# Another order of six units, and projections and weight-gradient pieces paced by a running sum

## The chip, the cores and the metric

One core of one Trainium2 chip runs the kernel as one program. The time is device microseconds. Before the change it is 910.07 us, the median of two runs (909.61 and 910.52). The engines are named as the profile names them: PE (TensorE, matmuls and transposes), ACT (ScalarE), DVE (VectorE), POOL (GpSimd) and SP, which issues DMAs.

## The reference

Forward and backward of a gated mix of two branches over 2048 tokens of width 512, all in bf16: `g = sigmoid(sum(x * gate_w))`, out = `g * A(x) + (1 - g) * B(x)`. A is sliding-window attention with 32 heads of width 16 and a window of 256 keys:

```
scores = einsum("bhqd,bhkd->bhqk", q, k) * Dh**-0.5
mask   = (i - j >= 0) & (i - j < 256)
p      = softmax(where(mask, scores, -1e9));  o = p @ v;  a = o @ wo
```

B is a gated feed-forward layer of width 1376 (`h = relu(x W_gate) * (x W_up)`, `b = h W_down`). The outputs are the mix and the gradients of x and of the six weights, for a given `grad_out`.

## The kernel before

The kernel has three stages. The feed-forward stage comes first, the attention stage (forward and backward in one sweep, from about 250 to 710 us) second, and a last stage makes the output and the gradient of x. The change touches the attention stage alone.

**Passes, blocks, units, turns.** The attention stage makes four passes c = 0 to 3, the four "head groups", of eight heads each. A pass goes over 16 blocks j of 128 queries. A block meets three key blocks: its own (role d, the diagonal), the one before (role m, the middle, wholly inside the window) and the one before that (role f, the far one). Each is handled in two halves of four heads, so a block is six units (two for j = 0, four for j = 1), and a pass is 90 units. One loop iteration n, a turn, starts unit n and carries older units on:

- `front`, turn n: PE makes the scores ST (128x512), ACT takes their exponential, POOL masks it for roles d and f (L695, L698);
- `front_dp`, turn n+1: PE makes dPT, the gradient of the probabilities;
- `gradp`, turn n+2: DVE multiplies the two (L712);
- `rowsum`, turn n+4: PE sums over keys into BA, eight small matmuls (L721, L723), and after a block's last unit ACT copies BA out (L727) and POOL makes the block's small tiles in four later turns;
- `flip`: the unit's two tiles are transposed for the key-side gradients. Roles d and m go through one DMA transpose per pair of halves, issued by SP. Role f goes through PE in turn n+4: eight transposes into a tile pt, 0.44 us of PE, copied out by ACT and DVE in turn (L72, L74). In pass 3 part of role m goes through PE too;
- `cd_piece`: PE adds finished blocks into CD, the gradients of k and v (L541, L544).

**Fill-in work.** While a group of four blocks runs, the next group's projections are made in six parts (`project_parts`): Q and dO (four matmuls of 512 columns each into a tile pp, evicted by DVE, L147 and L74, then spread by four DVE copies, L120), a DMA transpose, K and V (pp evicted by ACT, L72, then two masked copies on DVE, L169), and the transposes of K and V (ptp, evicted by DVE in two copies, L191 and L192). The gradient of wqkv of pass c-1 is made during pass c by `grad_parts`, 16 pieces of four matmuls each (wps, 0.65 us). Four pieces form one accumulation, so its tile is taken by the first piece and given back after the fourth. In passes 1 and 2 this tile comes from the ring TR, in pass 3 from the ring M.

**PSUM.** The eight banks are: M, four buffers (ST, dPT, and wps of pass 3); CD, one; BA, one; TR, two. TR serves pt, pp, ptp and, in passes 1 and 2, wps.

**What sets the order.** Instructions are written out by hand, turn by turn. A number `credit` rises by a fixed amount per turn and falls with each piece of fill-in work; a projection part or a gradient piece is written when credit allows. `held` is true while an accumulation has pieces left. While it is true, the next piece goes first, and the condition for a projection part asks for `not held`.

Of the kernel before, what the change touches and what calls it, by code (L numbers as in the profile page):

```python
# [22 lines left out]
def kernel(  # L23
# [32 lines left out]
    DC = D // P  # L56
# [3 lines left out]
    NTG = S // TGW  # L60
# [43 lines left out]
    NP = P // 32  # L104
# [7 lines left out]
    if True:  # L112
# [5 lines left out]
        def spread(gi, k):  # L118
            rows = slice(32 * k, 32 * k + 32)
            nc.vector.tensor_copy(zt[gi % ZB][rows, :, k, :, :].rearrange("p w t q -> p w (t q)"),  # L120
                                  proj[groups[gi]]["z"][rows, :, :])
# [76 lines left out]
    with ExitStack() as p1, tc.manual_schedule():  # L198
# [43 lines left out]
        half = TPG // 2  # L242
# [105 lines left out]
        for fc in range(FC):  # L348
            for tg in range(NTG):
                k = Step()  # L350
# [97 lines left out]
        for n in range(N1 + 8):  # L448
# [29 lines left out]
            if at(6):  # L478
                f = weights(at(6))
# [34 lines left out]
    if True:  # L514
# [68 lines left out]
        def clear(name):  # L583
            nc.gpsimd.memset(W6[(name, FC - 1)][0:FC * P - F, :], 0.0)
# [8 lines left out]
        def turns(name, src, k0, k1, tag):  # L593
            full, end = src.shape[1] // P, -(-src.shape[1] // P)
            ks = range(k0, min(k1, full))
            sets = [list(ks[i:i + 2]) for i in range(0, len(ks), 2)] + ([[full]] if k0 <= full < min(k1, end) else [])
            return [lambda s=s: turn_w(name, src, s, tag, s[0] - k0) for s in sets]

        def loads(name, src, k0, tag):
            def one(k):  # L600
                if (tag, "t") not in W6:
                    W6[(tag, "t")] = slot(tag)
                load_rows(name, src, k, W6[(tag, "t")][:, k - k0, :])
            return [lambda k=k: one(k) for k in range(k0, min(k0 + 4, FC))]
# [8 lines left out]
        def load_gw():  # L613
            nc.sync.dma_start(gw_b[:], gate_w.partition_broadcast(P))

        plan = {2: [load_gw], 5: turns("wqkv", A_wqkv, 0, 4, "p0"), 7: turns("wqkv", A_wqkv, 4, 8, "p1"),
                11: turns("wqkv", A_wqkv, 8, 12, "p2"),
                12: turns("Wg", B_W_gate, 0, 4, "x0") + turns("Wg", B_W_gate, 4, 8, "d0"),
                13: turns("Wg", B_W_gate, 8, 12, "x1") + turns("Wu", B_W_up, 0, 4, "d1") + [lambda: clear("Wg")],
                14: turns("Wu", B_W_up, 4, 8, "x2") + turns("Wu", B_W_up, 8, 12, "d2"),  # L620
                15: loads("Wd", B_W_down, 0, "x3") + [lambda: clear("Wu")] + loads("Wd", B_W_down, 4, "d3") + loads("Wd", B_W_down, 8, "p3") + [load_wo]}
# [35 lines left out]
        units = []  # L657
        for c in range(DC):
            for j in range(NT):
                kbs = [k for k in (j - 1, j, j - 2) if k >= 0]  # L660
                for half in range(2):
                    order = kbs if half or len(kbs) < 3 else [kbs[0], kbs[2], kbs[1]]
                    for ki, kb in enumerate(order):
                        u = Unit()
                        u.c, u.j, u.kb, u.half = c, j, kb, half
                        u.first = ki == 0 and half == 0
                        u.last = ki == len(kbs) - 1 and half == 1
                        u.role = ("d", "m", "f")[j - kb]
                        u.pair = u.role == "d" or (u.role == "m" and (c < DC - 1 or j in (3, 5, 7, 9)))
                        u.own = u.role == "f"  # L670
                        u.dma = u.pair or (u.role == "m" and half == 0 and (c < DC - 1 or j < 10))
                        units.append(u)
        NU = len(units)

        pairs = {}
# [172 lines left out]
        with tc.manual_schedule():  # L848
            ev = {}
            cdq = []  # L850
            bgq = []
            prq = []
# [3 lines left out]
            n = 0  # L856

            held = False
            fed = 1
            early = []  # L860
            late = []

            def background():
                f, more = bgq.pop(0)
                store = f()
                if store is not None:
                    copies.append(store)
                    if len(copies) > 2 or gi + 2 >= len(groups):
                        ev.setdefault(n + 2, []).append(("dma", flush))
                return more  # L870

            def flush():
                while copies:
                    copies.pop(0)()

            def pieces():
                nonlocal credit
                most = 2 if len(cdq) > 6 or (len(cdq) > 1 and cdq[1][5] and cdq[1][0] <= n and cdq[1][2] < NT - 1) else 1
                if u is not None and u.c == DC - 1 and u.j > 9 and w is not None:
                    most = 2 if w.dma else 1 if len(cdq) > 3 or cdq and cdq[0][5] else 0  # L880
                for _ in range(most):
                    if cdq and cdq[0][0] <= n:
                        cd_piece(*cdq.pop(0)[1:])
                        credit -= 0.2

            while n <= NU + LAG or ev or cdq or bgq:
                now = ev.pop(n, [])
                u = units[n] if n < NU else None
                if u is not None:
                    gi = u.c * NTG + u.j // TPG  # L890
                    if u.first and u.j == 0:
                        sts[u.c] = st.tile([P, NT, 4, P], BF, tag="rows_st", name="rows_st")
                    if u.first and u.j % TPG == 0:
                        if gi + 1 < len(groups):
                            prq = project_parts(*groups[gi + 1]) if gi else second
                            due = n + sum(2 * min(3, j + 1) for j in range(u.j, u.j + TPG)) - 3
# [24 lines left out]
                w = units[n - LAG] if LAG <= n < NU + LAG else None  # L921
# [28 lines left out]
                if n >= NU:  # L950
                    if bgq:
                        held = background()
                    elif n > NU + 1:
                        for _ in range(2):
                            if len(S2["grads"]) > DC:
                                S2["grads"].pop(0)()
                elif held and credit > 0.3:
                    held = background()
                    credit -= 0.65
                elif prq and not held and ((credit > 0.4 and n > fed + 1) or due - n <= len(prq)):  # L960
                    fed = n
                    credit -= (0.44, 0.86, 0.86, 0.1, 0.86, 0.86)[len(prq) - 1]
                    prq.pop(0)()
                    if len(prq) == 4:
                        for k in range(NP):
                            ev.setdefault(n + 1 + k, []).append(("dve", lambda gi=gi, k=k: spread(gi + 1, k)))
                        ev.setdefault(n + 1, []).append(("dma", flush))
                    if not prq:
                        late += plan.get(gi + 1, [])
                elif bgq and len(prq) <= 2 and credit > 0.3:  # L970
                    held = background()
                    credit -= 0.65
# [164 lines left out]
```

## Time and profile before

| quantity | us |
|---|---|
| median of the two runs | 910.07 |
| profiled execution, its own time | 911.05 |
| its span | 909.4 |
| PE busy | 895.0 (98%) |
| DVE / ACT / POOL busy | 511.8 / 441.3 / 491.7 |
| granted PE clock | 1.00 of full speed |

| pass | starts at us | lasts us |
|---|---|---|
| 0 | 251.7 | 101.9 |
| 1 | 353.6 | 115.5 |
| 2 | 469.1 | 115.9 |
| 3 | 585.0 | to about 703 |

The passes' starts are the starts of their first ST. The matmul rows are pipelined. A row of 128x512 reads 378 ns, while such matmuls that follow each other start 215 ns apart. So for PE this document reads the steps from start to start: 215 ns for 512 columns, 161 for 384 (wps), 55 for a transpose, 25 for the small ones of BA and CD. A step that is longer than its matmul's own is a wait of PE, and is called a stall below.

### The profile page before, as it was taken

What the parts mean: (1) busy time and instruction counts of PE and PEld (TensorE: products, weight loads), DVE (VectorE), ACT (ScalarE), POOL (GpSimd) and SP (SyncE); (2) the same over time, 40 slices, a digit from 0 to 9 for tenths busy, and PEclk for the clock granted to TensorE, in tenths of its full rate; (3) what the DMA queues carried; (4) which work ended last, traced back from release to release, by engine and by line L of the source; (5) the groups of instructions that cost most, each with busy time, mean ns of one, the idle gap of its engine ahead of it and who ended that gap; (6) DMA issues with size and microseconds to landing.
All of it is one profiled execution on the core that took longest, in us unless ns stands there. A gap on an engine that the chain in (4) does not pass through costs nothing.

```text
span 909.4 us, 26127 instructions
## 1 busy us (share of the span) xinstructions
PE 895.0 (98%) x10711; PEld 566.7 (62%) x10711; DVE 511.8 (56%) x952; ACT 441.3 (49%) x778; POOL 491.7 (54%) x937
## 2 busy tenths in 40 slices
PE   9999999999989999999999999999999999999998
PEld 5555656655657777667776677766777644444445
DVE  4433334324468887678886788876787222333223
ACT  6422232222278777667776677766788211100001
POOL 4644545545267778767777567875677312222221
PEclk9999999999999999999999999999999999999999
DMA  9998879999799999999999989999999998777731
GB/s 301 203 194 186 197 179 207 211 207 216 180 143 158 180 188 194 184 175 156 177 185 187 180 161 182 187 182 184 184 185 186 235 269 227 186 181 185 182 86 46
DMA packets 505575, 169.06 MB, mean 186 GB/s; under 512 B 433456, under 2 KB 504336, under 8 KB 505456
## 3 DMA queue, kind: packets, MB, share of 16 engines
q1 hardware_dynamic: 484816, 145.51, 86.8%
q10 hardware_dynamic: 19008, 17.31, 7.2%
q0 software_dynamic: 1632, 4.59, 1.4%
q8 instruction: 83, 1.36, 0.6%
q14 instruction: 36, 0.29, 0.1%
HBM read 32.28 MB, written 36.24 MB: 75 GB/s over the span
## 4 chain that ended last, share of the span: by engine, by line
PE 80%; DMA 5%; DVE 4%; POOL 3%; issue 3%; SPq 2%; ACT 2%; ACTq 0%; POOLq 0%; DVEq 0%
PE dxps L1062 8%; PE ST L683 8%; PE dPT L707 7%; PE pt L750 6%; PE wps L412 5%; PE wps L637 5%; PE dxps L1066 4%; PE CD L541 4%; PE bps L1035 4%; PE BA L721 4%; PE pp L133 4%; PE dps L414 3%; PE ups L363 3%; PE gps L363 2%; PE CD L544 2%
## 5 line engine op out<-in xcount | busy, mean ns | idle before, releaser
L683 PE MATMUL ST<-z,K 128*128 128x512 bf16 x360 | 135.8, 378 | 2.6 <-DVE PPm L712 1.2
L707 PE MATMUL dPT<-z,V 128*128 128x512 bf16 x360 | 136.0, 378 | 1.9 <-DVE Pd L712 0.5
L695 POOL TENSOR_SCALAR_AFFINE_SELECT PPd<-PPd 128x512 bf16<-128x512 bf16 x126 | 80.0, 635 | 86.7 <-ACT PPd L693 86.7
L377 POOL TENSOR_TENSOR hT<-rg,upm 128x512 bf16<-128x512 bf16 x44 | 51.8, 1176 | 116.0 <-DVE upm L375 104.3
L412 PE MATMUL wps<-dgu_r,x_r 128*128 128x256 bf16 (+1 forms) x704 | 103.9, 270 | 1.8 <-DVE wst L74 1.8
L712 DVE TENSOR_TENSOR PPd<-PPd,dPT 128x512 bf16<-128x512 bf16 x126 | 85.4, 678 | 18.3 <-PE dPT L707 9.1
L698 POOL TENSOR_SCALAR_AFFINE_SELECT Pu<-Pu 128x512 bf16<-128x512 bf16 x112 | 71.9, 642 | 31.8 <-ACT Pu L693 30.7
L412 PEld LDWEIGHTS <-x_r 128*128 128x128 bf16 x704 | 68.4, 98 | 33.1 <-issue 2.6
L712 DVE TENSOR_TENSOR Pd<-Pu,dPT 128x512 bf16<-128x512 bf16 x112 | 76.3, 681 | 21.5 <-POOL Pu L698 10.6
L693 ACT ACTIVATE PPd<-ST 128x512 bf16<-128x512 f32 x126 | 76.1, 605 | 22.0 <-PE ST L683 19.7
L712 DVE TENSOR_TENSOR PPm<-PPm,dPT 128x512 bf16<-128x512 bf16 x122 | 81.4, 668 | 7.8 <-PE dPT L707 6.1
L693 ACT ACTIVATE Pu<-ST 128x512 bf16<-128x512 f32 x112 | 67.4, 602 | 34.1 <-PE ST L683 33.6
L693 ACT ACTIVATE PPm<-ST 128x512 bf16<-128x512 f32 x122 | 73.7, 604 | 20.2 <-PE ST L683 19.6
L1042 ACT COPY a_sb<-aps 128x512 f32<-128x512 f32 x16 | 9.4, 586 | 151.4 <-issue 137.7
L375 DVE SCALAR_TENSOR_TENSOR upm<-rg,ups 128x512 bf16<-128x512 bf16 x44 | 30.1, 685 | 82.9 <-ACT rg L369 40.3
L369 ACT ACTIVATE rg<-gps 128x512 bf16<-128x512 f32 x44 | 26.3, 598 | 91.8 <-PE gps L363 44.2
L72 ACT COPY p<-pt 128x1024 bf16<-128x1024 bf16 x67 | 68.5, 1022 | 3.8
L414 PE MATMUL dps<-db_r,h_r 128*128 128x512 bf16 x176 | 66.7, 379 | 0.0
L387 POOL TENSOR_TENSOR dgu<-dh_sb,rg 128x512 bf16<-128x512 bf16 x44 | 56.7, 1289 | 5.3 <-ACT dh_sb L383 5.3
L1048 POOL DMA_DIRECT2D out_dram<-o_sb x16 | 8.7, 542 | 88.8 <-DVE o_sb L1046 82.4
L637 PE MATMUL wps<-rows_st,x_r 128*128 128x384 bf16 x256 | 50.3, 325 | 0.0
L133 PE MATMUL pp<-x,p 128*128 128x512 bf16 x192 | 49.0, 378 | 0.0
(193 smaller groups left out, 2357.5 us busy)
## 6 DMA issues: line engine op xcount, KB each, us to landing
dqkvo_d<-rows_st SPq DMA_DIRECT2D x15, 512.0 KB, 4.0
hT_d<-hT ACTq DMA_DIRECT2D x44, 128.0 KB, 2.5
dgT_d<-dgu ACTq DMA_DIRECT2D x44, 128.0 KB, 3.0
duT_d<-dgu ACTq DMA_DIRECT2D x44, 128.0 KB, 2.9
duT_g<-duT_d SPq DMA_DIRECT2D x8, 640.0 KB, 5.2
gt<-hT_d SPq DMA_DIRECT2D x7, 640.0 KB, 5.8
dgT_g<-dgT_d SPq DMA_DIRECT2D x7, 640.0 KB, 5.0
out_dram<-wst SPq DMA_DIRECT2D x20, 128.0 KB, 2.7
```

Source lines behind the costliest of these rows:

```text
L72: nc.scalar.copy(out, in_)
L133: nc.tensor.matmul(pp[:], lhsT=w_p[c][:, cd, which * P:(which + 1) * P], rhs=x_T[tg][:, cd, :], start=(cd == 0), stop=(cd == DC - 1))
L412: nc.tensor.matmul(acc["w"][:, c, 0:2 * nw], lhsT=x_r[:, t, c * P:(c + 1) * P], rhs=k.dgu_r[:, :, i, s0:P], start=(go_ and c % 2 == 0), st ...
L414: nc.tensor.matmul(acc["d"][:], lhsT=k.h_r[:, i, :], rhs=db_r[:, t, :], start=go_, stop=no_)
L637: nc.tensor.matmul(wps[:], lhsT=x_r[:, t, part * P:(part + 1) * P], rhs=sts[c][:, t, 0:3, :], start=first and t == t0, stop=last and t == ...
L683: nc.tensor.matmul(ST[:], lhsT=KTt[:, ksl], rhs=z[:, 0, :, jl, :], start=True, stop=True)
L693: nc.scalar.activation(u.Pu[:], ST[:], ACT.Exp)
L695: nc.gpsimd.affine_select(out=u.Pu[:], in_=u.Pu[:], compare_op=ALU.is_ge, fill=0.0, base=0, pattern=[[0, HH], [1, P]], channel_multiplier=-1)
L698: nc.gpsimd.affine_select(out=u.Pu[:], in_=u.Pu[:], compare_op=ALU.is_ge, fill=0.0, base=-1, pattern=[[0, HH], [-1, P]], channel_multiplier=1)
L707: nc.tensor.matmul(u.dPT[:], lhsT=VTt[:, ksl], rhs=z[:, 1, :, jl, :], start=True, stop=True)
L712: nc.vector.tensor_tensor(out=u.Pd[:], in0=u.Pu[:], in1=u.dPT[:], op=ALU.mult)
L1062: nc.tensor.matmul(to, lhsT=src[:, fc, lsl], rhs=W6[(wt, fc)][:, cols], start=(fc == 0 and wt == "Wg"), stop=False)
```

## The change

It has two parts. First, the six units of a block get another order. With m0 for the middle key block and the first half, it was m0 f0 d0 m1 d1 f1, and is m0 m1 f0 d0 d1 f1. For block 1 it was m0 d0 m1 d1 and is m0 m1 d0 d1. Second, in passes 0, 1 and 2 the fill-in work is written by a new rule in place of `credit`: `todo` counts the parts and pieces that the pass still has, `phase` rises each turn by `todo` over the turns left (from 2 in pass 0, 18 parts; in passes 1 and 2, 20 parts and 16 pieces), and one part or piece is written when phase reaches 1, at least two turns after the last one, and not in a turn with PE transposes unless phase is over 1.5. A projection part goes before a gradient piece, whatever `held` says. Pass 3 keeps the old rule. No instruction is added or taken out.

```diff
-                kbs = [k for k in (j - 1, j, j - 2) if k >= 0]
-                for half in range(2):
-                    order = kbs if half or len(kbs) < 3 else [kbs[0], kbs[2], kbs[1]]
-                    for ki, kb in enumerate(order):
...
+                order = [(k, h) for k, h in ((j - 1, 0), (j - 1, 1), (j - 2, 0), (j, 0), (j, 1), (j - 2, 1)) if k >= 0]
+                for kb, half in order:
...
+            def project():
+                nonlocal fed, late, todo
+                fed = n
+                todo -= len(prq) != 4
+                prq.pop(0)()
+                if len(prq) == 4:
+                    for k in range(NP):
+                        ev.setdefault(n + 1 + k, []).append(("dve", lambda gi=gi, k=k: spread(gi + 1, k)))
+                    ev.setdefault(n + 1, []).append(("dma", flush))
+                if not prq:
+                    late += plan.get(gi + 1, [])
...
+                elif u.c < DC - 1:
+                    if u.first and u.j == 0:
+                        todo = 5 * NTG - (2 if u.c == 0 else 0) + (16 if u.c else 0)
+                    phase = min(1.6, phase + todo / max(4, (u.c + 1) * (NU // DC) - n - 2))
+                    turn = len(prq) == 4
+                    if prq and (turn and n > fed + 1 or due - n <= len(prq)):
+                        project()
+                        phase -= not turn
+                    elif phase >= 1 and (w is None or w.dma or phase > 1.5) and n > fed + 1 and (prq and not turn or bgq):
+                        phase -= 1
+                        if prq:
+                            project()
+                        else:
+                            fed = n
+                            todo -= 1
+                            held = background()
                 elif held and credit > 0.3:
                     held = background()
                     credit -= 0.65
                 elif prq and not held and ((credit > 0.4 and n > fed + 1) or due - n <= len(prq)):
-                    fed = n
                     credit -= (0.44, 0.86, 0.86, 0.1, 0.86, 0.86)[len(prq) - 1]
-                    prq.pop(0)()
...
+                    project()
```

## Prediction

> **What bounds the kernel now.** I read the engines' line first, then busy time by pass, then the timeline of PE around one block. In the engines' line the reader sees that PE is busy nearly all of the span and that nothing else comes near.
>
> ```profile
> PE 895.0 (98%) x10711; PEld 566.7 (62%) x10711; DVE 511.8 (56%) x952; ACT 441.3 (49%) x778; POOL 491.7 (54%) x937
> ```
>
> The windows below are the stage's first four blocks, the rest of pass 0, and passes 1, 2 and 3. After the stretch come its length, then busy time of PE, PEld, DVE, ACT and POOL.
>
> ```profile
> 251.70:270.10 18.40, 16.00 (x204) 9.60 (x203) 12.66 (x26) 14.42 (x27) 12.39 (x29) 1.00 0.82 139
> 270.10:353.60 83.50, 83.39 (x1563) 59.98 (x1561) 68.88 (x130) 66.64 (x119) 64.82 (x152) 1.00 1.07 178
> 353.60:469.10 115.50, 115.03 (x2011) 81.00 (x2007) 89.29 (x168) 83.65 (x150) 84.83 (x197) 1.00 1.09 176
> 469.10:585.00 115.90, 115.05 (x2011) 80.86 (x2008) 90.44 (x168) 83.14 (x149) 84.78 (x197) 1.00 1.09 180
> 585.00:703.00 118.00, 116.36 (x2087) 84.59 (x2084) 88.85 (x162) 86.95 (x153) 83.94 (x195) 1.00 1.11 184
> ```
>
> PE idles 5.5 us here (451.3 less 445.8). Its rows overlap, so the start-to-start steps are the better reading. Summed over what each step exceeds its own length (215, 161, 55 or 25 ns), the stalls are 5.1 us in pass 0 (4.1 of it in the first four blocks), 1.9 in pass 1, 2.3 in pass 2 and 2.8 in pass 3: 12.0. The Trainium skill ("Trainium Kernel Development and Optimization", section Performance Expectations) says matmul busy time is a bad metric, because matmuls are pipelined. It is so here: by busy time 5.5 us are to be won, by steps 12.0.
>
> So the stage is a string of PE instructions with hardly a gap. An edit that adds no instruction can win at most those 12.0 us (1.3%), and any new wait of PE is paid in full.
>
> **What the change moves.** On every engine the changed program has the same instructions in another order. I cost it by the work of PE per block: 48 steps of 25 ns of BA, 48 of CD, 12 of 215 ns, 16 transposes of 55 ns are 5.86 us; a projection part adds 0.86, the transposes of K and V 0.44, a gradient piece 0.65.
>
> Pass 0: before, blocks 8 to 11 carry 7.58, 8.02, 5.86, 5.86; after 7.58, 6.72, 6.72, 6.30. That is flatter. Passes 1 and 2: before, blocks 3 to 7 take 9.32, 8.87, 8.65, 9.30, 6.94, and blocks 10, 11, 14, 15 the bare 5.86; after, 6.54, 7.58, 7.58, 7.59, 7.15 and 7.79, 7.15, 7.79, 7.79. Blocks 8, 9, 12 and 13 keep 7.58 and 8.02: their projection parts stand in the same turns as before. Only gradient pieces move.
>
> Does the flattening help? The bare blocks of before last 5.90 to 6.05 us against 5.86 of work, so they cost almost nothing now: ACT, DVE and POOL keep up even there. What is there to win is the stalls behind projection parts (0.10 to 0.25 us in blocks 5, 9 and 13, 0.15 in the next, 0.6 to 1.1 in block 2 of passes 1 and 2), where products wait for DVE. I take half of the 5.1 us that passes 0 to 2 lose behind their start: **-2.6** (ends 0 and -5.1). The first four blocks get one projection part less and the transposes of K and V later: 0 (between -1 and +1.5, as their 4.1 us of stalls take up most of either). Pass 3 gets its PE transposes in adjoining turns, but two TR banks are free there: 0 (between -1 and +1).
>
> The m pairs' DMA transposes are issued two turns earlier on SP, the d pairs' in the same turn; the waits of PE name no DMA, so 0. The four masks of a block (L695, L698, 0.64 us each) now stand in adjoining turns, and POOL's small ops, 3.1 us a block, fall mostly in the other two: 5.7 us of POOL in at least 5.9, as before: 0.
>
> **What the change adds.** The new rule lets projection parts run while an accumulation is open. In passes 1 and 2 the accumulation's tile is one of the two TR banks. In the order of the changed program a first piece is written in block 3 and the accumulation ends in block 7; the next opens at block 7, position 4, and ends in block 10; the next opens in block 11 and ends in block 14. So **all projections of blocks 4 to 6, 8 to 9 and 12 to 13 share the one other bank with the blocks' own transposes pt.** Before, the accumulation's four pieces ran without a projection between them, and the least work of PE between two uses of a bank by pt, pp or ptp was 1.9 us.
>
> A use of a bank must wait until the last one is evicted. The timeline of pass 1, blocks 8 and 9, has the pieces (PE, then DVE, then ACT; start and length in us):
>
> ```profile
> 416.84 1.02 PE L136 MATMUL pp<-d,p 128*128 128x512 bf16 x4
> 417.70 0.38 PE L683 MATMUL ST<-z,K 128*128 128x512 bf16 x1
> 418.13 0.38 PE L750 MATMUL pt<-ident,Pu 128*128 128x128 bf16 x4
> ...
> 417.90 0.69 DVE L74 CAST zT<-pp 128x512 bf16<-128x512 f32 x1 [0.86 <-PE pp L136]
> ...
> 420.74 1.01 ACT L72 COPY p<-pt 128x1024 bf16<-128x1024 bf16 x1
> ```
>
> The dO part's steps end at 417.70, its eviction starts 0.20 us later and ends at 418.59. pt starts at 418.13, in the other bank. With one bank it waits to 418.64 (0.05 us to wake PE, as at 660.73, where DVE ends p2m, and 660.78, where pt starts). **A hand-off thus takes 0.25 us plus the eviction, less the work of PE between.** That work is 0.415 us in the closest case (ST and BA ahead of pt, or dPT and CD ahead of pp), and 1.04 or more in the others. The evictions, from the groups by line:
>
> ```profile
> L72 ACT COPY p<-pt 128x1024 bf16<-128x1024 bf16 x67 | 68.5, 1022 | 3.8
> L74 DVE COPY p<-pt 128x1024 bf16<-128x1024 bf16 x45 | 30.8, 684 | 7.9 <-PE pt L750 7.5
> L74 DVE CAST zT<-pp 128x512 bf16<-128x512 f32 x16 | 11.1, 692 | 11.9 <-PE pp L136 11.9
> L72 ACT CAST VT<-pp 128x512 bf16<-128x512 f32 x16 | 9.4, 587 | 7.8 <-PE pp L133 7.8
> ```
>
> The new unit order makes the closest case frequent: f0 moves from position 1 to 2, so its pt moves from a block's last turn to its first, where Q and K are written in blocks 8, 9, 12 and 13. Per pass the changed order has:
> - pp right behind pt, evicted by ACT (blocks 8, 9, 12, 13, position 0): 4 x (0.25 + 1.02 - 0.415) = 3.42;
> - pt right behind dO (blocks 8 and 12): 2 x (0.25 + 0.69 - 0.415) = 1.05;
> - pt right behind K or V (block 5; 9 and 13): 3 x (0.25 + 0.587 - 0.415) = 1.27;
> - twelve with 1.04 to 1.45 us between: 0 (at most 0.04) where the evicting engine is free at once.
>
> That is 5.74 per pass, **+11.5** for two. DVE isn't always free. In block 9 of before its copy of pt starts at 427.46, 1.0 us behind the transposes' end at 426.45, not 0.20. There (blocks 9 and 13, ptp behind pt) the hand-off takes 1.0 + 0.68 + 0.05 less 1.04, some 0.7, less the 0.4 that PE has just lost waiting for V: 0.3 each. In block 5, V comes behind a pt whose copy stands behind two masked copies of K (0.48 each) and a product (0.60 from start to start): about 0.85. That is 1.45 per pass, **+2.9** for two (between 0 and 10, the latter if the nine evictions by DVE per pass with at most 1.25 us behind them all come 0.6 us late).
>
> Sum: 911.05 - 2.6 + 11.5 + 2.9 = 922.85 for the profiled execution. That is 0.98 above the median, so **922** for the median, 1.3% slower.
>
> **Rivals.**
> 1. *Waiting on DVE spreads.* DVE works its rows off in the program's order, so an eviction that waits for a late pp holds up the products behind it, and the products hold up PE. It decides when DVE's backlog outgrows the roughly one turn (1.05 us) that products have in hand. For it: in blocks 9 and 13 DVE has some 9.2 us of work (six products, a copy of pt, three spreads of 0.56, four masked copies, 1.7 in all, the eviction of ptp, 0.9, a reciprocal) against 8.0 of PE. Against: before has the same load in blocks 9 and 13 and stalls 0.25 us; and each new stall lets DVE catch up. With +10 in place of +2.9, and nothing won: 910 + 11.5 + 10 = 931; I take 927 to 935. Chance 0.13.
> 2. *The flattening wins.* Place: the stalls behind projection parts in passes 0 to 2. Price: all 9.2 us of those passes, 901. It decides if the open accumulation does not block the second bank. Against: two buffers are all that TR has, and the written order leaves it open across the projections. Chance 0.09.
> 3. *The waits are partly covered,* because evictions start earlier or the 5.1 us vanish entirely: 911 + 11.5 - 5.1 - 1, with some of the hand-offs halved, 911 to 916. Chance 0.08. That the change doesn't do what it says (the late groups keep their bunched projections) lies in this case too: the hand-offs stay.
> 4. *No overlap at all.* Work between two uses hides nothing: all 28 or so hand-offs per pass cost their eviction, 21.6 us a pass: 951. The trace speaks against it, since 0.415 us of work stands between even in the closest case. Chance 0.01. The Trainium skill ("Perfetto Trace Analysis", section Matmuls) has the rule behind it: independent groups should rotate through different banks, so that an eviction overlaps the next group's matmuls. The trace of before agrees where two banks turn (pt at 418.13, 0.46 us ahead of the end of the eviction); no run yet shows the one-bank case.
>
> **How the numbers follow.** Forecast 0.69 at 922 (its own range 916 to 927), rivals 0.13, 0.09, 0.08 and 0.01. The range 914 to 931 leaves out rival 2, most of the upper half of rival 1 and part of 3: 0.18. A measurement of this kernel tells about 2% (18 us) from no change. Faster by over 2% needs more than all stalls of the stage: 0.01. Slower by over 2% (above 928.3) is most of rival 1, rival 4 and the forecast's tail: 0.13. Within 2%: 0.86.
>
> **What would show it.** In the changed profile, pp waits for ACT's copy of pt in blocks 8, 9, 12 and 13 (0.85 us each, eight in all), pt for zT, KT or VT (0.4 to 0.5 us), ptp for DVE's copy. Passes 1 and 2 last about 121 us each, pass 0 101 to 102, pass 3 as now. If passes 1 and 2 grow without those waits, or pt and pp start without them, the reason is wrong. If ST and dPT wait for DVE instead, it is rival 1.

## The result

The changed kernel takes **923.64 us**, the median of two runs (923.25 and 924.03), against 910.07 before. The ratio is 1.0144, with a 95% interval from 1.0127 to 1.016: slower by 13.6 us, clear of the measurement's noise and under the 2% mark. The prediction was 922.

### The profile page after: what moved, and what is told of

It is laid out like the page before. It is cut to its first block, busy times and chain, and to the rows that moved or that the text cites. A ratio compares the mean times of both kernels' runs of the same rounds, so it can differ in the third digit from the quotient of the medians.

```text
span 921.5 us, 26148 instructions
## 1 busy us (share of the span) xinstructions
PE 899.6 (98%) x10711; PEld 568.9 (62%) x10711; DVE 511.0 (55%) x952; ACT 443.6 (48%) x778; POOL 494.0 (54%) x937
## 5 line engine op out<-in xcount | busy, mean ns | idle before, releaser
L710 DVE TENSOR_TENSOR PPd<-PPd,dPT 128x512 bf16<-128x512 bf16 x126 | 82.6, 672 | 13.0 <-POOL PPd L693 6.8
L710 DVE TENSOR_TENSOR PPm<-PPm,dPT 128x512 bf16<-128x512 bf16 x122 | 81.8, 681 | 12.1 <-PE dPT L705 10.2
L72 ACT COPY p<-pt 128x1024 bf16<-128x1024 bf16 x61 | 62.2, 1020 | 3.8 <-PE pt L748 0.6
L386 DVE TENSOR_TENSOR dgu<-dh_sb,upm 128x512 bf16<-128x512 bf16 x44 | 33.7, 766 | 30.3 <-ACT dh_sb L383 27.0
```

Source lines behind the costliest of these rows:

```text
L72: nc.scalar.copy(out, in_)
L710: nc.vector.tensor_tensor(out=u.Pd[:], in0=u.Pu[:], in1=u.dPT[:], op=ALU.mult)
```

## Profile after

The profiled execution took 923.25 us, with a span of 921.5. The engines' line again, then busy time in the same five stretches (first four blocks, rest of pass 0, passes 1, 2 and 3). After the stretch come its length and busy time of PE, PEld, DVE, ACT and POOL.

```profile
PE 899.6 (98%) x10711; PEld 568.9 (62%) x10711; DVE 511.0 (55%) x952; ACT 443.6 (48%) x778; POOL 494.0 (54%) x937
```

```profile
250.58:268.01 17.43, 15.67 (x196) 8.90 (x195) 12.46 (x25) 14.12 (x26) 11.18 (x27) 1.00 0.92 148
268.01:352.16 84.15, 84.03 (x1560) 60.41 (x1560) 67.39 (x131) 66.59 (x118) 66.09 (x154) 1.00 1.11 181
352.16:474.32 122.16, 116.51 (x2011) 81.57 (x2007) 89.11 (x168) 84.17 (x150) 85.31 (x197) 1.00 1.03 171
474.32:596.65 122.33, 116.53 (x2011) 81.56 (x2007) 89.56 (x168) 83.55 (x149) 85.29 (x196) 1.00 1.00 169
596.65:714.65 118.00, 116.31 (x2083) 84.65 (x2080) 88.67 (x161) 87.25 (x153) 84.79 (x195) 1.00 1.10 182
```

Pass 0 keeps its length (101.6 us, before 101.9). Passes 1 and 2 grow from 115.5 and 115.9 to 122.2 and 122.3, with the same 2011 matmuls: 13.1 us together, nearly all of the 13.6. PE is still 98% busy, so the engines' line shows nothing of it. The waits of PE in passes 1 and 2 do. The columns are who waited, for whom, the total in us, how many times, and the longest. Before, one row was all there was:

```profile
PE ST L683 <- DVE PPm L712: 1.2, 2, 0.6
```

After:

```profile
PE pp L133 <- ACT p L72: 6.0, 8, 0.8
PE pt L748 <- DVE zT L74: 1.5, 4, 0.4
PE pt L748 <- ACT VT L72: 1.1, 4, 0.3
PE ptp L176 <- DVE p L74: 0.8, 4, 0.2
PE pt L748 <- ACT KT L72: 0.5, 2, 0.3
PE pp L133 <- DVE p L74: 0.4, 2, 0.2
PE ST L681 <- DVE PPd L710: 0.3, 2, 0.2
PE CD L541 <- POOL rq L774: 0.2, 1, 0.2
```

The first six rows are the hand-offs of one TR bank, with the counts that the prediction took from the order: eight, four, six (four for V and two for K), four, two. A row of the waits leaves out the up to 0.16 us by which a matmul's modelled end overhangs its step; by start-to-start steps the same waits are 7.19, 2.09, 2.49, 1.42 and 0.71 us, with 0.13 of a kind too short for this list: 14.0.

One of the eight in the timeline, pass 1, block 9. The rows are PE's and then ACT's; the first two columns are start and length in us, and the bracket at the end is the idle time ahead and its releaser:

```profile
415.52 0.39 PE L748 MATMUL pt<-ident,Pd 128*128 128x128 bf16 x4
415.74 0.38 PE L705 MATMUL dPT<-z,V 128*128 128x512 bf16 x1
...
417.06 1.02 PE L133 MATMUL pp<-x,p 128*128 128x512 bf16 x4 [0.75 <-ACT p L72]
...
416.00 1.01 ACT L72 COPY p<-pt 128x1024 bf16<-128x1024 bf16 x1
```

The transposes' steps end at 415.74, ACT's copy runs from 416.00 to 417.01, and K's projection starts 0.05 us later. Without the wait it would have started 0.415 us behind the transposes, at 416.16: a loss of 0.90. Before, the same projection started in the very us in which the copy still ran (421.74 against a copy from 420.74 to 421.75), because it had the other bank.

## The experiments

Three readings were open. The theory: an accumulation that stays open across projections holds one bank of a ring of two. The rivals: the moved load (DVE and ACT come late wherever the work stands), and the unit order by itself. The table has all kernels. "Passes 1+2" is from the first ST of pass 1 to the first of pass 3 in the profiled execution, "TR waits" the stalls in front of pp, pt and ptp there, by steps, and "others" all other stalls of those two passes.

| kernel | us, median | ratio to before | interval | passes 1+2 | TR waits | others |
|---|---|---|---|---|---|---|
| before | 910.07 | | | 231.4 | 0.0 | 4.2 |
| changed | 923.64 | 1.0144 | 1.0127 to 1.016 | 244.5 | 14.0 | 3.2 |
| order alone | 910.68 | 1.0012 | 1.0002 to 1.0022 | 231.0 | 0.0 | 3.8 |
| pacing alone | 924.22 | 1.0159 | 1.0143 to 1.0174 | 243.6 | 12.2 | 4.2 |
| accumulations closed first | 908.88 | 0.9989 | 0.998 to 0.9999 | 230.4 | 0.0 | 3.3 |
| the same, again | 908.77 | 0.9981 | 0.9973 to 0.9989 | 230.4 | 0.0 | |
| parts kept apart | 915.37 | 1.0059 | 1.0044 to 1.0074 | 235.7 | 5.4 | 3.2 |
| closed and apart | 911.16 | 1.0014 | 1.0005 to 1.0023 | 231.5 | 0.0 | 4.9 |
| copies swapped | 929.0 | 1.0206 | 1.0189 to 1.0224 | 250.1 | 18.4 | 4.4 |
| before, accumulations open | 912.98 | 1.0034 | 1.002 to 1.0047 | 234.4 | 3.2 | 4.0 |
| tile from ring M | 926.7 | 1.0181 | 1.0163 to 1.02 | 247.2 | 0.0 | 20.0 |
| old order, closed | 912.26 | 1.0021 | 1.0009 to 1.0032 | 232.1 | 0.0 | |

The profiles of "the same, again" and "old order, closed" lack some 100 of 10711 matmul rows, whose absence looks like stalls. Stalls other than named waits are left out for those two.

### Each part alone

The order alone is the kernel before with the new list of units:

```diff
-                kbs = [k for k in (j - 1, j, j - 2) if k >= 0]
...
+                order = [(k, h) for k, h in ((j - 1, 0), (j - 1, 1), (j - 2, 0), (j, 0), (j, 1), (j - 2, 1)) if k >= 0]
```

> The kernel before with only the new unit order; pacing by credit as before. Theory (one TR bank): every accumulation of gradient pieces is closed before a projection part is written, so both TR banks turn and no use of a bank has less than 1.9 us of work since the last one: no hand-off costs anything, 910 us (908 to 912). Rival (the unit order costs by itself, by four masks of POOL or two m halves in a row): most of the 13.6 us stay, 918 to 924.

Measured: 910.68 us, 0.8 above the 909.87 of before on the same chip. The order costs next to nothing by itself: the rival falls.

This kernel shows more than was asked of it. In blocks 8, 9, 12 and 13 of passes 1 and 2 its transposes and projection parts stand in the same turns as in the changed kernel, with Q and K right behind the transposes that ACT copies out. No accumulation is open there, and PE waits for none of them. Here is K in pass 1, block 9 (PE, then ACT):

```profile
421.92 0.39 PE L748 MATMUL pt<-ident,Pd 128*128 128x128 bf16 x4
422.56 1.02 PE L133 MATMUL pp<-x,p 128*128 128x512 bf16 x4
...
422.40 1.01 ACT L72 COPY p<-pt 128x1024 bf16<-128x1024 bf16 x1
```

The projection starts 0.16 us after the copy begins, in the other bank. In the changed kernel the same neighbours cost 0.90 us.

The pacing alone is the changed kernel with the old list of units (the same diff the other way round).

> The changed kernel with the old unit order; the new pacing in passes 0 to 2. Theory: accumulations stay open across the projections of three groups per pass. pt now stands in a block's turns 3 and 5, so Q and K no longer follow a pt, but pt follows dO (0.52), K or V (0.42) and the transposes of K and V (0.73, DVE's two copies 0.9) directly, three times each per pass: 5.05 us per pass, 10.1 for two, about 920 (917 to 924) if DVE is late at some of them. The three pp behind pt (0.85 each) must not appear. Rival (only both parts together cost): 910 to 912. Rival (the loss is the moved load, not the bank): as the changed kernel, 922 to 925, with PE waiting at ST and dPT.

Measured: 924.22 us, as slow as both parts together, and 0.2 above the upper end of what was expected. By the time alone, the rival of the moved load (922 to 925) fits better; the places of the waits decide. Its waits of PE in passes 1 and 2:

```profile
PE pt L750 <- DVE KV L192: 2.9, 6, 0.5
PE pt L750 <- DVE zT L74: 2.3, 6, 0.4
PE pt L750 <- ACT VT L72: 1.6, 6, 0.3
PE ptp L176 <- DVE p L74: 1.3, 6, 0.2
PE BA L721 <- ACT BAs L727: 0.9, 2, 0.5
PE CD L541 <- ACT rows_st L547: 0.5, 2, 0.2
PE ST L683 <- DVE PPm L712: 0.3, 2, 0.2
```

The three kinds that were named stand there six times each, and no pp stands behind ACT's copy of pt in the list. By steps they are 3.81, 3.14 and 2.48 us (9.4, expected 10.1), and ptp behind a late DVE adds 2.1, which the expectation had left open. ST and dPT wait no more than before (1.7 us by steps against 3.1), so the moved load doesn't show here. So the new order isn't needed for the loss; it only decides which neighbours meet in the one bank. Some 2 us more of the loss lie outside passes 1 and 2: pass 0 takes 103.5 us here.

### Closing the accumulations first

The changed kernel with one rule more in the new branch:

```diff
+                    if held and prq:
+                        fed = n
+                        todo -= 1
+                        phase -= 1
+                        held = background()
-                    if prq and (turn and n > fed + 1 or due - n <= len(prq)):
+                    elif prq and (turn and n > fed + 1 or due - n <= len(prq)):
```

> The changed kernel with one rule more: when a new group's projections are at hand and an accumulation is open, its left pieces (at most three) are written first, one a turn. Unit order and pacing otherwise as changed. Theory: no projection part lies inside an open accumulation, both TR banks turn, hand-offs cost 0. The flattening is left with what it wins: 908 to 911. Rival (moved load on DVE and ACT, or the unit order, is the cause): 919 to 924.

Measured: 908.88 us, 14.8 less than the changed kernel and 1.0 less than before on the same chip. One wait of PE is left in the list of passes 1 and 2:

```profile
PE ST L681 <- DVE PPd L710: 0.3, 2, 0.2
```

The same units and the same rule for the pace, with the accumulation closed first: this takes the loss away whole. The rule moves projection parts too, though. In pass 1 Q goes from the first turn of block 8 to the second of block 9, and no Q or K stands right behind a pt any more. So this run alone doesn't tell the free bank from the changed neighbours. The order alone does, which keeps the neighbours and has no wait, and so does the run with another ring below, which keeps every turn. It was run again beside the kernel with the old order:

> The kernel with accumulations closed before projections, but with the old unit order. Theory (the bank is all there is): no part lies inside an open accumulation, hand-offs 0: 909 to 911, that is e2_pace less some 14 us. Rival (the old order needs the credit rule, so that e2_pace's loss has another cause): 917 to 924. Against the next kernel it also tells whether the new order has a part in the gain of closing: if so it is 1 to 2 us slower than that one.

> The kernel with accumulations closed before projections, as in e3_close, beside the old order on the same chip. Theory: 908.5 to 909.5 against 909.9 of before, a ratio of 0.9985 to 0.9995; rival: no difference from before, the ratio's interval holds 1.

Measured: 912.26 us with the old order (1.0009 to 1.0032 of before) and 908.77 with the new one (0.9973 to 0.9989). Closing takes 12.0 us off the pacing with the old order, as it takes 14.8 off with the new. The first ends 1.3 us above what was expected, and 3.5 above the second: with the pacing in place, the new order is worth that much, of which passes 1 and 2 show 1.7 (232.1 against 230.4) and pass 0 1.9 (103.5 against 101.6). Why the old order loses there wasn't tested.

So there is a version that beats both kernels: the one before by 1.0 to 1.5 us, the changed one by some 15. The first is what the pacing and the new order are worth together once the bank is free. The pacing alone doesn't win: with the old order the closed kernel is 2.0 us slower than before.

### Open accumulations, but apart from the transposes

```diff
-                    phase = min(1.6, phase + todo / max(4, (u.c + 1) * (NU // DC) - n - 2))
+                    phase = min(4.0, phase + todo / max(4, (u.c + 1) * (NU // DC) - n - 2))
...
-                    elif phase >= 1 and (w is None or w.dma or phase > 1.5) and n > fed + 1 and (prq and not turn or bgq):
+                    elif phase >= 1 and (w is None or w.dma and (not prq or units[n + 1 - LAG].dma)) and n > fed + (1 if prq else 0) and (prq and not turn or bgq):
```

> The changed kernel, accumulations still open across projections (two per pass, each over five parts), but a projection part is never written in a turn with PE transposes nor in the turn before; gradient pieces may follow in the next turn, and the running sum is capped at 4 in place of 1.6. Theory: one bank is used in those stretches, but at least 1.04 us of PE work stands between two uses, so the closest hand-offs (0.42 to 0.85 us each) are gone: 910 to 914, the rest being hand-offs that wait for a late DVE. Rival (an open accumulation costs by itself, wherever the parts stand): 918 to 924.

Measured: 915.37 us, 1.4 us above the expected range. What is left stands in its waits:

```profile
PE pp L133 <- DVE p L74: 3.2, 4, 0.8
PE ptp L176 <- DVE p L74: 0.6, 4, 0.2
PE ST L681 <- DVE PPd L710: 0.3, 2, 0.2
```

The hand-offs by ACT and those behind zT, KT and VT are gone, as the theory has it. Left are K's projection and ptp behind a pt that DVE copies. The 1.04 us of PE work between would be enough for a free DVE; but DVE is late. In pass 1, block 9, the transposes' steps end at 419.36, and DVE still has a spread of zT (from 419.54) and a product (from 420.00) ahead, so that its copy starts at 420.60. The four waits of K's projection are 0.94 us each by steps. So an open accumulation costs through the hand-offs, and a late evicting engine can make one out of a whole turn's distance.

The two rules together (closed and apart):

> The kernel with accumulations closed before projections, and in addition no projection part in a turn with PE transposes nor in the turn before. Theory: nothing is left for the second rule to win once two banks turn: 908 to 910, as with closing alone. Rival (parts next to transposes cost something of their own, by DVE's queue): 905 to 907.

Measured: 911.16 us, 2.3 above closing alone, and against both readings: keeping the parts apart costs when two banks turn. BA then waits for DVE's products (1.1 us, five times in the waits of passes 1 and 2), so parts crowd in other turns and DVE comes late there. That reading is argued from those rows, not tested.

### The cause alone, in the kernel before

Order and credit as before; only the priority of projections over an open accumulation is new (passes 0 to 2):

```diff
-                elif held and credit > 0.3:
-                    held = background()
-                    credit -= 0.65
-                elif prq and not held and ((credit > 0.4 and n > fed + 1) or due - n <= len(prq)):
+                elif prq and not (held and u.c == DC - 1) and ((credit > 0.4 and n > fed + 1) or due - n <= len(prq)):
...
+                elif held and credit > 0.3:
+                    held = background()
+                    credit -= 0.65
```

> The kernel before, unit order and pacing by credit as they were, but in passes 0 to 2 a projection part goes ahead of an open accumulation's next piece. Theory: two accumulations per pass now have projection parts inside, and pt comes directly behind dO (0.52), K (0.42) and the transposes of K and V (0.73) once each per pass: 3.4 us for two passes, with a late DVE up to 5: 913 to 915. Rival (an open accumulation is harmless without the new order and the flattening): 909 to 911.

Measured: 912.98 us, 3.1 above the 909.86 of before on that chip, with 3.15 us of TR waits. The median lies 0.02 under the expected range. Three hand-offs were named and three appear, two each, but one stands behind V's eviction where K's had been named:

```profile
PE ST L683 <- DVE PPm L712: 1.2, 2, 0.6
PE pt L750 <- DVE KV L192: 1.0, 2, 0.5
PE pt L750 <- DVE zT L74: 0.8, 2, 0.4
PE pt L750 <- ACT VT L72: 0.5, 2, 0.3
```

The first row is old; the other three are new. The cause works without the other parts of the change, and its price is the sum of its hand-offs.

### The same turns, another ring

Every instruction stays in its turn; only the ring that gives the accumulation its bank changes:

```diff
-                    own, tag, bufs = (ps, "M", 4) if c + 2 >= DC else (psr, "TR", 2)
+                    own, tag, bufs = (ps, "M", 4)
```

> The changed kernel, every instruction in the same turn, but the accumulation's tile comes from the ring M in passes 1 and 2, as it does in pass 3. Theory: TR keeps two banks, its hand-offs (7.0 us a pass) vanish. ST and dPT have three banks left over 15 to 20 turns, so a dPT's bank must be free within about one turn, and they wait wherever DVE is late: I estimate 1 to 4 us a pass, 911 to 918, with the waits at ST and dPT and none at pp, pt or ptp. Rival (the loss comes with the moved work, whatever bank the accumulation holds): 922 to 925.

Measured: 926.7 us. The first half of the theory held: no wait at pp, pt or ptp is left. The second was far off: ST and dPT wait instead, 15.8 us more in two passes than before, where 2 to 8 had been estimated.

```profile
PE ST L681 <- ACT PPm L691: 2.3, 6, 0.4
PE dPT L705 <- DVE PPm L710: 2.2, 6, 0.4
PE dPT L705 <- ACT Pu L691: 2.0, 4, 0.5
PE dPT L705 <- DVE Pd L710: 1.4, 4, 0.4
PE ST L681 <- ACT Pu L691: 0.7, 2, 0.4
```

With three banks, ST and dPT wait for ACT's exponentials and for DVE's products, in turn after turn. In total time this looks like the rival, moved work that costs whatever bank is held. The places of the waits say otherwise. K's projection in pass 1, block 9, stands where it stood in the changed kernel, and starts 0.84 us before the copy of pt ends:

```profile
416.12 1.01 ACT L72 COPY p<-pt 128x1024 bf16<-128x1024 bf16 x1
...
416.29 1.02 PE L133 MATMUL pp<-x,p 128*128 128x512 bf16 x4
```

So what costs is that a bank is held at all for some 20 turns (19 to 21 in pass 1), and the ring it is taken from decides who waits.

### The price of a hand-off, by swapping the copies

```diff
-            eng = ("act", "dve", "act")[copier["i"] % 3] if u.c == 0 else ("act", "dve")[copier["i"] % 2]
+            eng = ("act", "dve", "act")[copier["i"] % 3] if u.c == 0 else ("act", "dve")[(copier["i"] + (u.c < DC - 1)) % 2]
```

> The changed kernel with the two engines that copy pt swapped in passes 1 and 2: in a block's first turn DVE (0.68 us) in place of ACT (1.02), in its fourth turn ACT in place of DVE. Theory (a hand-off costs 0.25 plus the eviction less the work between): the eight pp behind pt fall from 0.90 to 0.56 each; pp or ptp behind the other pt (1.04 us between) go from 0.35 to 0.22, and dO in block 4 gets 0.22: per pass 5.4 in place of 7.0, together -3.1, about 920.5 (919 to 922). Rival (the waits are set by how late DVE is, not by the copy's length): no gain or a loss, 923 to 927.

Measured: 929.0 us, 5.4 slower than the changed kernel instead of 3.1 faster. The shorter copy made it worse. By steps, Q's projection waits 0.53 us behind DVE's copy in blocks 8 and 12, as worked out. K's, in blocks 9 and 13, waits 2.13 three times and 1.74 once (DVE, then PE, pass 1, block 9):

```profile
416.41 0.88 DVE L120 COPY z<-zT 32x1024 bf16<-32x1024 bf16 x1
417.32 0.69 DVE L710 TENSOR_TENSOR PPd<-PPd,dPT 128x512 bf16<-128x512 bf16 x1
418.04 0.43 DVE L120 COPY z<-zT 32x1024 bf16<-32x1024 bf16 x1
418.51 0.69 DVE L74 COPY p<-pt 128x1024 bf16<-128x1024 bf16 x1
...
416.48 0.39 PE L748 MATMUL pt<-ident,Pd 128*128 128x128 bf16 x4
416.71 0.38 PE L705 MATMUL dPT<-z,V 128*128 128x512 bf16 x1
419.25 1.02 PE L133 MATMUL pp<-x,p 128*128 128x512 bf16 x4 [1.98 <-DVE p L74]
```

The transposes are through at 416.71, but DVE's copy starts at 418.51: two spreads of zT and a product stand ahead of it. The rival was right here: a hand-off takes the evicting engine's backlog plus the copy, and the backlog, 1.80 us here, was over two and a half times the copy.

## Why the prediction was right

- **The bound.** The stage is a string of PE instructions, and a new wait is paid in full. The stalls of passes 1 and 2 grew by 13.1 us (17.26 less 4.17), their length by 13.1, the kernel by 13.6.
- **The closest hand-offs.** Predicted 11.5. Measured 7.19 (eight pp behind pt, 0.90 each against 0.855), 2.09 (four, 0.52) and 2.49 (six, 0.415): 11.8. Count, place and price held.
- **Hand-offs behind a late DVE.** Predicted 2.9: 0.3 for each ptp, 0.85 for V in block 5. Measured 0.355 for every one, 2.1 in all. V's term was mis-sized by more than half: the 0.42 us that pt had just waited for KT, which the prediction took off for ptp, it didn't take off there.
- **What the flattening wins.** Predicted -2.6. The other stalls fell by 0.95 us in passes 1 and 2 and rose by 0.15 in pass 0 and 0.07 in pass 3: -0.7. This is the step that was furthest off, by 1.9 us. "Half of the 5.1 us" was a choice between two ends without a row behind it. The closed version, at 1.0 to 1.5 us below before, agrees with the smaller figure, though its parts stand in other turns.
- **Zero terms.** The order of the units: 0.8 us by itself (interval 0.2 to 2.0). The first four blocks took no longer than before (17.4 us against 18.4). The reason given for this term was misread: the traces have two projection parts and the transposes of K and V there in both kernels, and what is less after the change is eight transposes into pt, 0.44 us. Pass 3 lasts 0.5 us longer from its first ST to its last CD matmul, since one unit's transposes (0.44 us) move there from pass 2. The DMAs of the m pairs showed no wait.
- **The sum.** 14.0 less 0.7 is 13.3 of stalls, against 11.8 predicted. The span grew by 12.1 only, as the stage began 1.1 us earlier in this execution (250.58 against 251.70). That start lies between 249.6 and 252.1 in the twelve profiles, also of kernels that share every earlier instruction. The term for a late DVE (0.8 too high) and that for the gain (1.9 too good) partly cancel, and the early start takes off more: that the profiled execution's 923.25 lies 0.4 from the predicted 922.85 is luck. By the medians, the loss was 13.6 against 11.9 predicted.
- **The rivals.** Spreading waits on DVE (rival 1) didn't occur in the changed kernel: ST and dPT wait no more than before. Even with the copies swapped, where a late DVE held up K's projection, ST and dPT waited 2.3 us by steps, against 3.1 before. The winning flattening (rival 2) needed the bank to be free, and even then brought 1.0 to 1.5 us, not 9.2. Rival 3 is out: the closest hand-offs were paid in full, at 0.90, 0.52 and 0.415 us. Rival 4's 951 is out: where 1.04 us or more lay between two uses, at most 0.36 us each was paid. The Trainium skill ("Perfetto Trace Analysis", section Matmuls) asks for rotating banks so that evictions overlap the next group's matmuls; the traces agree in kind, at 14.0 us of waits with one bank and none with two.

## What to carry to other kernels

An accumulation in pieces holds its PSUM bank from the first piece to the eviction. Before other work is put between its pieces, one should count what else uses that ring and what PE work lies between two uses: a hand-off costs the time until the evicting engine starts (0.20 us here when it was free, 1.80 with a backlog), plus the eviction, plus some 0.05 us, less that work. In this kernel, with PE 98% busy, the pacing and the new order brought little (1.0 to 1.5 us of 910), and a bank tied up brought a loss some ten times as large.

## What the runs showed beside this

In the kernel with swapped copies, K's projection waited 2.13 us three times and 1.74 us once. Behind the first of these waits the granted clock fell to half, from 420.50 to 423.91 us; the columns after the five engines are the clock, the DMA share and GB/s.

```profile
417.00:420.50 3.50, 1.52 (x21) 0.85 (x20) 2.10 (x4) 0.19 (x1) 2.79 (x8) 1.00 0.45 94
420.50:424.00 3.50, 3.50 (x47) 1.85 (x44) 1.81 (x4) 1.87 (x4) 1.00 (x2) 0.51 1.06 193
```

By steps this cost 1.3 us: a matmul of 512 columns took 380 to 427 ns in place of 215, but most of the small ones of BA and CD 26 to 30 in place of 25. The Trainium skill ("TensorE: Matmul & The Clock Gate", Part 1) describes a free-running window of about 3.4 us whose being idle halves the clock. The length agrees, at 3.41 us; but the window wasn't wholly idle.

The traces show how much was enough. In this one the clock changes on a grid of 3.41 us: the change before 420.50 lies at 10.89, 120 such steps back. In the step that ends at 420.50, PE's rows leave 1.98 us idle. The other three waits fall so that no step holds more than 1.68 us of idle time, and the clock stayed at 1.00. Counted over all twelve traces, from each one's first record of full speed on, three steps have 1.83 us idle or more, and half speed followed each of them. The longest idle time in any other step is 1.79 us, and half speed followed none of those. No experiment set out to test this.
